# Routing attention with an FFN on one core: the checks of the row sums move behind the next turn's exponentials in the first batch

## The chip, the cores and the metric

The kernel runs on one core of a Trainium2 chip. The metric is the device time of one execution in microseconds (us), taken as the median of several runs; less is better. The profile shows one further execution, instruction by instruction. Engines are named as there: PE is TensorE (matrix products; PEld is its weight load), DVE is VectorE, ACT is ScalarE, POOL is GpSimd, SP is SyncE, whose queue issues nearly all DMA transfers. Each engine works through its own instructions in a fixed order and waits on semaphores for the others.

## The reference

Attention by clusters, for 4 batches of 8 heads, 768 positions and 64 dimensions, and then a two-layer network with a quick GELU on the 3072 rows of 512 values.

```python
q_assign = np.argmax(np.einsum('bhsd,hcd->bhsc', q_n, c_n), axis=-1)   # 16 centroids a head
k_assign = np.argmax(np.einsum('bhsd,hcd->bhsc', k_n, c_n), axis=-1)
mask = q_assign[:, :, :, None] == k_assign[:, :, None, :]
scores = np.where(mask, scale * np.matmul(q, k.transpose(0, 1, 3, 2)), -1e9)
attn = np.exp(scores - np.max(scores, axis=-1, keepdims=True))
attn = attn / (np.sum(attn, axis=-1, keepdims=True) + 1e-09)
x = np.matmul(attn, v)            # then (B,H,S,D) -> (B*S, H*D)
h = x @ w_in                      # 512 -> 2048
g = h * (1.0 / (1.0 + np.exp(-1.702 * h)))
out = g @ w_out                   # 2048 -> 512
```

The weights come as 64-bit floats, q, k, v and the centroids as 32-bit floats.

## The kernel before, in words

`fast` computes everything without subtracting the row maximum. To be safe it takes, for every group of rows, the reciprocals of the row sums and checks them: `check(g)` (L472) makes two ACT passes over the tile `rec` (128 x 384). The first copies it and adds it up (L476), the second applies a Relu with a bias and adds that up (L478). Both sums go to `sums`, which is read near the end; if a sum is out of bounds, `general` computes everything anew (L33 to L35).

**Groups and turns.** Two heads of one batch make a pair (16 pairs, four to a batch). Each pair has two halves of 384 query rows, so there are 32 groups g. A group takes six units u, one for each tile of 128 keys: `scores(u)` (L386, PE, 2 heads), `part(u)` (L398, the mask as a further product, in the first batch only), `exps(u)` (L412, ACT, L417), `mask(u)` (L420: in the first batch only POOL's running sum of the exponentials, L438; from the second batch on also DVE's masking, L428), `values(u)` (L442, PE, L449; after the sixth unit ACT copies the result at L454). Two units make a turn t, so a group has three turns (TG = 3) and a batch 24 (TB = 24). The loop over the turns (L597 to L638) writes the instructions out by hand, and that is the order in which each engine works.

**One turn t**, in the order of the code: the scores and `part` of its two units; their exponentials; in the second half of the first batch and later (`second_half`, t >= 12) one round of weight conversion (L609); `check` of whatever group has been normalised and not yet checked (L610, L611); `mask`; centroid products of a coming pair, if they are due (`prep_near`, whose ACT copy is L290); `values` of the turn before; every third turn (t = 4, 7, 10, 13, ...) `normalise(g)` for the group that has just been completed, before the preparation steps when t >= 12 (L625) and after them otherwise (L629); the preparation steps of coming pairs (`prep_turn`: three PE transposes at L270 and one ACT copy at L275 each; `prep_assign` on DVE, L295 to L324); the check again, when t < 24 (L630, L631); a round of weight conversion (L633); chunks of the network (`first`, L513, with tanh at L485 and a DVE product at L486; `second`, L491, with ACT's scaling at L496); and a further round (L638) in odd turns with t >= 12.

**Normalising** (L456): PE adds POOL's sums over the partitions with a product by ones (L461), DVE takes the reciprocal straight from PSUM (L464) and multiplies the group's result by it (L466). `rec` is one of three rotating tiles `short` that also hold the products of `prep_near` and a step of `prep_assign`.

**Weight conversion.** A round (L190) loads a chunk (L154, SP), splits another (DVE L167 and L169, then ACT L171 and L173) and joins the one before (DVE L179, L182, L185). There are 32 chunks, all in the first batch's stage.

**PSUM.** Three banks `m` rotate among the transposes, the centroid products, the row sums of L461, the network's chunks and its outputs (`bank()`, L106). Two double banks `s` hold the scores: the scores of a turn can't start before the exponentials of the turn before have read theirs.

**After the first batch** the same loop goes on for three batches, with chunks of the network as filling; then the rest of the network is computed with seven products instead of eight (L696 to L728).

Of the kernel before, what the change touches and what calls it, by code (L numbers as in the profile page):

```python
# [18 lines left out]
def kernel(  # L19
    tc: tile.TileContext,  # L20
    q: bass.AP,
    k: bass.AP,
    v: bass.AP,
    centroids: bass.AP,
    moe_w_in: bass.AP,
    moe_w_out: bass.AP,
    out: bass.AP,
):

    args = (q, k, v, centroids, moe_w_in, moe_w_out, out)
    bad = fast(tc, *args)  # L33
    with tc.If(bad > 0):
        general(tc, *args)  # L35
# [3 lines left out]
def fast(  # L39
# [150 lines left out]
    def round_next():  # L190
        i = w_done[0]
        if i < NW:
            load_w(i + 2)
            split_w(i)
        if 0 < i <= NW:
            join_w(i - 1)
        w_done[0] += 1
# [188 lines left out]
    def scores(u):  # L386
        g, kt = divmod(u, NJ)
        p, h = split(g)
        ps = ps_s.tile([P, 2, 512], FP32, name="s")
        for a in range(2):  # L390
            rows = slice(a * D, (a + 1) * D)
            nc.tensor.matmul(out=ps[:, a, 0:HALF],  # L392
                             lhsT=T[p, 1][rows, kt * P:(kt + 1) * P],
                             rhs=T[p, 0][rows, h * HALF:(h + 1) * HALF],
                             start=True, stop=(p >= HP))
        s_of[u] = ps[:, :, 0:HALF]

    def part(u):  # L398

        g, kt = divmod(u, NJ)  # L400
        p, h = split(g)
        if p >= HP:
            return
        for a in range(2):
            r = 32 * (2 * (p % 2) + a)
            nc.tensor.matmul(
                out=s_of[u][:, a, :],
                lhsT=hots[p // 2, 1][r:r + NC, kt * P:(kt + 1) * P],
                rhs=hots[p // 2, 0][r:r + NC, h * HALF:(h + 1) * HALF],
                start=False, stop=True)  # L410

    def exps(u):  # L412
        p, h = split(u // NJ)
        s = s_of[u]
        if p < HP:
            A_of[u] = ap.tile([P, 2, HALF], FP32, name="A")
        nc.scalar.activation(out=A_of[u] if p < HP else s, in_=s, func=AF.Exp,  # L417
                             scale=SCALE)

    def mask(u):  # L420

        g, kt = divmod(u, NJ)
        p, h = split(g)
        s = s_of.pop(u)
        if p >= HP:
            A_of[u] = ap.tile([P, 2, HALF], FP32, name="A")
            for a in range(2):
                nc.vector.scalar_tensor_tensor(  # L428
                    out=A_of[u][:, a, :],
                    in0=qcode[p][:, a, h * HALF:(h + 1) * HALF],  # L430
                    scalar=code[p][:, kt % NH, 1, kt // NH, a:a + 1],
                    in1=s[:, a, :], op0=ALU.is_equal, op1=ALU.mult)
        A = A_of[u]
        if kt == 0:
            return
        if kt == 1:
            sum_of[g] = ap.tile([P, 2, HALF], FP32, name="sum", bufs=2)
        nc.gpsimd.tensor_tensor(out=sum_of[g],  # L438
                                in0=A_of[u - 1] if kt == 1 else sum_of[g],
                                in1=A, op=ALU.add)  # L440

    def values(u):  # L442
        g, kt = divmod(u, NJ)
        p, h = split(g)
        if kt == 0:
            o_of[g] = ps_o.tile([P, 512], FP32, name="o")
        A = A_of.pop(u)
        for a in range(2):
            nc.tensor.matmul(out=o_of[g][a * D:(a + 1) * D, 0:HALF],  # L449
                             lhsT=v_in[p][:, a, kt, :], rhs=A[:, a, :],  # L450
                             start=(kt == 0), stop=(kt == NJ - 1))
        if kt == NJ - 1:
            O_of[g] = xp.tile([P, HALF], FP32, name="x")
            nc.scalar.copy(O_of[g], o_of.pop(g)[:, 0:HALF])  # L454

    def normalise(g):  # L456

        sm = sum_of.pop(g)
        ps = bank()
        for a in range(2):  # L460
            nc.tensor.matmul(out=ps[a * D:(a + 1) * D, 0:HALF], lhsT=ones,  # L461
                             rhs=sm[:, a, :], start=True, stop=True)
        rec = recs[g] = short()
        nc.vector.reciprocal(out=rec, in_=ps[:, 0:HALF])  # L464
        x = xT_of[g] = O_of.pop(g)
        nc.vector.tensor_tensor(out=x, in0=x, in1=rec, op=ALU.mult)  # L466
        if g % HP == HP - 1 and g < 2 * HP:
            (half_ffn, ffn)[g // HP].extend((ffn_half, ffn_tiles)[g // HP]())

    recs = {}  # L470

    def check(g):  # L472


        rec = recs.pop(g)
        nc.scalar.activation(out=rec, in_=rec, func=AF.Copy,  # L476
                             accum_out=sums[:, 0, g:g + 1])
        nc.scalar.activation(out=rec, in_=rec, func=AF.Relu, bias=top[:, 0:1],  # L478
                             scale=-2.0 * LIMIT * LIMIT,
                             accum_out=sums[:, 1, g:g + 1])  # L480
# [86 lines left out]
    TB = 2 * HP * TG  # L567

    prep_at = {}
    for p in range(1, NPAIR):  # L570
        b, hp = divmod(p, HP)
        for i in range(2 if p == 1 else 0, len(PREP)):
            if p == 1:
                t = (i - 2) // 2
            elif b == 0:
                t = (hp - 2) * TG + 1 + i // 2
            else:
                t = b * TB + TG * hp - (7, 7, 6, 6, 4, 3, 2)[i]
# [5 lines left out]
    def prep(p, i):  # L584
        if i == 0 and p:
            load_v(p)
        PREP[i](p)
        if i in (1, 3) and loads:
            load_qk(*loads.popleft())
# [7 lines left out]
    for t in range(NT + 2):  # L597
        us = range(2 * t, 2 * t + 2) if t < NT else ()
        for u in us:
            scores(u)  # L600
        if t == 0:
            prep(0, 6)
        for u in us:
            part(u)
        for u in us:
            exps(u)
        second_half = t >= TB // 2
        if second_half:
            round_next()  # L609
        if recs:  # L610
            check(*recs)  # L611
        for u in us:
            mask(u)
        work = sorted(prep_at.get(t, ()), key=lambda w: PREP[w[1]] != prep_near)
        while work and PREP[work[0][1]] == prep_near:
            prep(*work.pop(0))
        if 1 <= t <= NT:
            for u in range(2 * t - 2, 2 * t):
                values(u)

        todo = half_ffn or (ffn if len(ffn) > NF // 2 else ())
        owed += (rate if half_ffn else 0.62) if todo else -owed
        g = (t - 2) // TG if t >= 2 and (t - 2) % TG == TG - 1 else None
        if g is not None and second_half:
            normalise(g)  # L625
        for p, i in work:
            prep(p, i)
        if g is not None and not second_half:
            normalise(g)  # L629
        if recs and t < TB:  # L630
            check(*recs)  # L631
        if second_half or t and t % 4 != 3:
            round_next()  # L633
        while owed >= 1 and todo:
            todo.popleft()()
            owed -= 1
        if second_half and t % 2:
            round_next()  # L638
# [565 lines left out]
```

## Time and profile before

| what | value |
|---|---|
| median of 5 runs | 1081.89 us (1081.7 to 1084.53) |
| the profiled execution's own time | 1081.72 us |
| its span, first to last instruction | 1079.9 us |
| PE busy | 1028.3 us (95%) |
| DVE busy | 600.3 us (56%) |
| ACT busy | 359.5 us (33%) |
| POOL busy | 296.4 us (27%) |
| mean granted PE clock | 0.984 |
| check, first pass L476 (32 of them, whole span) | 0.52 us and 0.19 us to read its sum |
| check, second pass L478 | 0.62 us and 0.19 us |
| ACT's idle time before L476, waiting for L466, 40 to 216 us | 24.7 us in 7 waits |
| first seven checks, start of L476 | 44.23, 63.12, 77.47, 99.03, 133.25, 166.18, 207.88 us |

The span counts from the first to the last instruction; the execution's own time has 1.8 us around it. A share of busy time is an average over the whole span, and the first batch, which takes some 230 us, differs much from what follows. In a timeline, a row gives the start, the duration, the engine, the line, the operation, the tiles (out<-in) and in brackets how long the engine had been idle and what ended that. fp32 products appear as two records each. Where neighbouring rows overlap a little, instructions are pipelined.

### The profile page before, as it was taken

To read this page: it belongs to the slowest core of one execution; us is meant where nothing else is said; L and a number is where in the kernel's file an instruction comes from. 1 tells how busy PE (TensorE), PEld (TensorE's weight loads), DVE (VectorE), ACT (ScalarE), POOL (GpSimd) and SP (SyncE) were. 2 spreads that over 40 slices of the span, in tenths; PEclk is the share of its full clock that TensorE was granted. 3 is DMA by queue.
4 is the path that set the end of the run, shared out by engine and by line. 5 is a ranking of instruction groups with operands and counts; after the bars stand their busy time and mean duration, and the time that the engine had idled before them with its cause. 6 is when DMAs were issued, how large, how long until landed. Compare 5 with 4: busy or idle time off the path is not lost. (4 is left out here: it accounts for less than half of the span.)

```text
span 1079.9 us, 11138 instructions
## 1 busy us (share of the span) xinstructions
PE 1028.3 (95%) x4142; PEld 502.0 (46%) x4142; DVE 600.3 (56%) x912; ACT 359.5 (33%) x649; POOL 296.4 (27%) x168
## 2 busy tenths in 40 slices
PE   7878798999999999999998999999999999999997
PEld 3323354345544455444543455444555444555443
DVE  3899998326876787667877866400366200565000
ACT  3654464324545555555554122100122000122000
POOL 2555222224665657655667000000000000000000
PEclk9998899999999999999999999999999999999999
DMA  7523354112003310221000000000000000000000
GB/s 195 143 64 112 117 162 127 47 39 69 9 15 73 97 31 1 59 67 40 9 1 1 10 1 1 10 20 19 11 1 0 10 19 20 10 1 1 20 20 22
DMA packets 64817, 45.18 MB, mean 42 GB/s; under 512 B 51952, under 2 KB 57584, under 8 KB 64752
## 3 DMA queue, kind: packets, MB, share of 16 engines
q1 hardware_dynamic: 64608, 44.33, 14.3%
q8 instruction: 35, 0.57, 0.2%
q14 instruction: 30, 0.25, 0.1%
q10 hardware_dynamic: 144, 0.03, 0.0%
HBM read 38.04 MB, written 6.31 MB: 41 GB/s over the span
## 5 line engine op out<-in xcount | busy, mean ns | idle before, releaser
L438 POOL TENSOR_TENSOR sum<-sum,A 128x768 f32<-128x768 f32 x128 | 235.7, 1841 | 201.3 <-DVE A L428 104.5
L491 PE MATMUL m<-w_out,gb 128*128 128x512 f32 x576 | 247.7, 592 | 0.0
L708 DVE TENSOR_TENSOR gb<-b,gb 128x384 f32<-128x384 f32 x168 | 93.4, 556 | 214.9 <-PE b L703 208.3
L428 DVE SCALAR_TENSOR_TENSOR A<-qb,code,s 128x384 f32<-128x384 uint8 x288 | 157.6, 607 | 94.8 <-ACT s L417 79.7
L491 PEld LDWEIGHTS m<-w_out,gb 128*128 128x128 f32 x576 | 109.4, 190 | 137.1 <-issue 136.6
L392 PE MATMUL s<-T,T 64*128 64x384 f32 x768 | 158.8, 526 | 13.2 <-ACT A L417 9.0
L449 PE MATMUL o<-A,inv 128*64 128x384 f32 x768 | 146.9, 502 | 1.1 <-DVE A L428 1.1
L417 ACT ACTIVATE s<-s 128x768 f32<-128x768 f32 x144 | 109.4, 794 | 83.3 <-PE s L392 72.6
L392 PEld LDWEIGHTS s<-T,T 64*128 64x128 f32 x768 | 66.2, 189 | 86.4 <-issue 24.0
L496 ACT ACTIVATE y<-m 128x512 f32<-128x512 f32 x24 | 14.3, 596 | 261.6 <-PE m L491 238.6
L485 ACT ACTIVATE th<-gb 128x768 f32<-128x768 f32 x48 | 40.4, 842 | 170.0 <-DVE gb L708 140.0
L464 DVE RECIPROCAL short<-m 128x384 f32<-128x384 f32 x32 | 81.6, 2551 | 13.6 <-PE m L461 13.5
L449 PEld LDWEIGHTS o<-A,inv 128*64 128x64 f32 x768 | 47.1, 137 | 86.4 <-issue 81.2
L438 POOL TENSOR_TENSOR sum<-A 128x768 f32<-128x768 f32 x32 | 59.4, 1857 | 93.4 <-ACT A L417 43.9
L703 PE MATMUL b<-x,S 128*128 128x384 f32 x192 | 69.8, 486 | 0.0
L703 PE MATMUL b<-T,w_in 128*128 128x384 f32 x192 | 69.8, 486 | 0.0
L703 PE MATMUL b<-x,w_in 128*128 128x384 f32 x192 | 66.3, 486 | 0.0
L513 PE MATMUL m<-x,w_in 128*128 128x384 f32 x128 | 51.2, 558 | 15.7 <-ACT short L290 4.9
L491 PE MATMUL m<-w_out,g 128*128 128x512 f32 x120 | 58.6, 613 | 0.2 <-ACT T L275 0.2
L486 DVE SCALAR_TENSOR_TENSOR gb<-th,gb 128x768 f32<-128x768 f32 x48 | 45.7, 953 | 21.8 <-ACT th L485 21.8
L542 PEld LDWEIGHTS m<-x,w_in 128*128 128x128 f32 x384 | 44.7, 192 | 11.2 <-issue 10.2
L542 PE MATMUL m<-x,w_in 128*128 128x128 f32 x384 | 48.8, 280 | 0.5 <-ACT T L275 0.5
(95 smaller groups left out, 862.8 us busy)
## 6 DMA issues: line engine op xcount, KB each, us to landing
raw<-in_moe_w_in_dram SPq DMA_DIRECT2D x16, 512.0 KB, 3.7
raw<-in_moe_w_out_dram SPq DMA_DIRECT2D x16, 512.0 KB, 3.6
in<-in_q_dram SPq DMA_DIRECT2D x32, 192.0 KB, 2.9
in<-in_k_dram SPq DMA_DIRECT2D x32, 192.0 KB, 3.5
inv<-in_v_dram SPq DMA_DIRECT2D x16, 384.0 KB, 4.3
out_dram<-y SPq DMA_DIRECT2D x24, 256.0 KB, 2.0
qb<-line SPq DMA_DIRECT2D x12, 192.0 KB, 3.3
line<-row SPq DMA_DIRECT2D x12, 1.5 KB
```

The costliest lines, as they stand in the source:

```text
L392: nc.tensor.matmul(out=ps[:, a, 0:HALF], lhsT=T[p, 1][rows, kt * P:(kt + 1) * P], rhs=T[p, 0][rows, h * HALF:(h + 1) * HALF], start=True, ...
L417: nc.scalar.activation(out=A_of[u] if p < HP else s, in_=s, func=AF.Exp, scale=SCALE)
L428: nc.vector.scalar_tensor_tensor(out=A_of[u][:, a, :], in0=qcode[p][:, a, h * HALF:(h + 1) * HALF], scalar=code[p][:, kt % NH, 1, kt // NH ...
L438: nc.gpsimd.tensor_tensor(out=sum_of[g], in0=A_of[u - 1] if kt == 1 else sum_of[g], in1=A, op=ALU.add)
L449: nc.tensor.matmul(out=o_of[g][a * D:(a + 1) * D, 0:HALF], lhsT=v_in[p][:, a, kt, :], rhs=A[:, a, :], start=(kt == 0), stop=(kt == NJ - 1))
L464: nc.vector.reciprocal(out=rec, in_=ps[:, 0:HALF])
L486: nc.vector.scalar_tensor_tensor(out=g, in0=t, scalar=1.0, in1=h, op0=ALU.add, op1=ALU.mult)
L491: nc.tensor.matmul(out=ps[:, 0:DM], lhsT=g, rhs=w_out[:, f, :], start=(f == 0), stop=(f == NF - 1))
L513: nc.tensor.matmul(out=ps[:, 0:HALF], lhsT=w_in[:, c, f * P:(f + 1) * P], rhs=xT[c], start=(c == 0), stop=(c == NCH - 1))
L542: nc.tensor.matmul(out=ps[:, f % 2 * P:(f % 2 + 1) * P], lhsT=w_in[:, c, f * P:(f + 1) * P], rhs=xT[c][:, n * P:(n + 1) * P], start=(c == ...
L703: nc.tensor.matmul(out=ps[:, 0:HALF], lhsT=a(c), rhs=x(c), start=(c == 0), stop=(c == 1))
L708: nc.vector.tensor_tensor(out=o, in0=a, in1=b, op=ALU.add)
```

## The change

One condition and its call go. After it the check at L610 and L611 is the only one in the loop, so a group normalised in turn t is checked in turn t + 1, behind that turn's exponentials (and behind the round at L609, where there is one). Groups 7 to 31 were checked there already; groups 0 to 6, normalised in turns 4, 7, 10, 13, 16, 19 and 22, were checked in the turn of their normalisation.

```diff
@@ -627,8 +627,6 @@
             prep(p, i)
         if g is not None and not second_half:
             normalise(g)
-        if recs and t < TB:
-            check(*recs)
         if second_half or t and t % 4 != 3:
             round_next()
         while owed >= 1 and todo:
```

The lines behind it have numbers smaller by two in the changed kernel; line numbers in the text are those of the kernel before, unless a row of the changed kernel is shown.

## The prediction

> **What bounds the kernel now.** I read the page's slices first, then busy time by stretch, then the instructions of each engine in order of time from 40 to 220 us, where the moved checks stand. The slices: one digit is the busy share of 27 us in tenths.
>
> ```profile
> PE   7878798999999999999998999999999999999997
> DVE  3899998326876787667877866400366200565000
> PEclk9998899999999999999999999999999999999999
> ```
>
> PE is at 9 from the eighth slice (189 us) on. The seven slices before it are the only stage in which PE has slack, and in it DVE stands at 8 or 9 from the second slice on. All seven moved checks lie there (44.2 to 209.3 us). The stretches (columns: length, busy us and instructions of PE, PEld, DVE, ACT, POOL, granted clock, DMA share, GB/s):
>
> ```profile
> 137.20:172.60 35.40, 35.40 (x167) 17.78 (x166) 33.00 (x50) 21.46 (x41) 10.15 (x6) 1.00 0.48 146
> 172.60:177.60 5.00, 0.16 (x2) 0.00 (x0) 4.97 (x5) 2.21 (x5) 3.62 (x2) 0.98 0.36 105
> 177.60:184.50 6.90, 6.84 (x17) 3.94 (x18) 4.08 (x8) 2.50 (x6) 0.00 (x0) 0.77 0.84 239
> 217.00:1080.00 863.00, 845.05 (x3283) 418.35 (x3281) 434.69 (x677) 249.02 (x448) 218.71 (x121) 1.00 0.08 22
> ```
>
> PE's last long stop is 172.6 to 177.6, while DVE works without a pause; from 177.6 on PE is full and DVE is not. So the time is: how long DVE and ACT need until they let PE go at 177.6, and PE's own work after that. An earlier gain counts only if it shortens DVE's chain up to there; a delay of PE after that is paid in full.
>
> Four timelines (start, duration, engine, line, operation, and in brackets the idle time before with what ended it). ACT: the check of turn 7 with the exponentials of turn 8; the end of turn 20; turn 23.
>
> ```profile
> 59.53 0.81 ACT L364 ACTIVATE qb<-m 64x768 bf16<-64x768 bf16 x1
> 63.12 0.52 ACT L476 ACTIVATE short<-short 128x384 f32<-128x384 f32 x1 [2.77 <-DVE x L466]
> ...
> 64.29 0.19 ACT L478 ACTIVATION_READ_ACCUMULATOR short<-short,top 128x1 f32 x1
> 64.50 1.51 ACT L417 ACTIVATE A<-s 128x768 f32<-128x768 f32 x2
> ...
> 174.67 0.72 ACT L171 ACTIVATE e<-e,low 128x512 int32<-128x512 int32 x1 [1.57 <-DVE e L167]
> 176.61 0.63 ACT L173 ACTIVATE w_out<-w_out 128x512 f32<-128x512 int32 x1 [1.22 <-DVE w_out L169]
> 177.15 0.46 ACT L290 COPY short<-m 128x384 f32<-128x384 f32 x1
> ...
> 215.12 0.49 ACT L290 COPY short<-m 128x384 f32<-128x384 f32 x1
> ```
>
> ```profile
> 65.36 2.93 PE L392 MATMUL s<-T,T 64*128 64x384 f32 x8 [3.01 <-ACT A L417]
> ...
> 171.89 0.87 PE L270 MATMUL m<-ident,in 128*128 128x128 f32 x6
> 177.66 6.98 PE L513 MATMUL m<-x,w_in 128*128 128x384 f32 x16 [4.90 <-ACT short L290]
> ...
> 215.94 0.87 PE L270 MATMUL m<-ident,in 128*128 128x128 f32 x6
> ```
>
> ```profile
> 65.72 1.93 DVE L167 TENSOR_SCALAR e<-raw 128x512 int32<-128x512 int32 x1
> 67.57 2.04 DVE L169 TENSOR_SCALAR w_in<-raw 128x512 int32<-128x512 int32 x1
> ```
>
> ```profile
> 65.45 3.87 POOL L438 TENSOR_TENSOR sum<-sum,A 128x768 f32<-128x768 f32 x2 [2.78 <-ACT A L417]
> ```
>
> At 59.53 ACT has nothing more to do but the check, and the check waits for the reciprocal; the exponentials of turn 8, whose scores are ready at 60.9, stand behind it, and PE waits 3.01 us for them. That is the wait which the change takes away. The last two fences show a second coupling: L167 and L169 take 0.42 us elsewhere and 1.9 to 2.0 us beside a row sum of POOL. Between 44 and 177 us, 20 DVE instructions are lengthened so, by some 1.55 us each.
>
> **Moved.** Seven checks (turns 4, 7, 10, 13, 16, 19, 22), two ACT instructions each with their accumulator reads. Start to start a check takes ACT 1.26 us (44.23 to 45.49). Nothing is added or removed; the order of PE, DVE, POOL and the SP queue is unchanged. On ACT each check goes past the weight splits (L171, L173), tanh (L485) or output scaling (L496) at the end of its turn, and the next turn's exponentials; in turns 14, 17 and 20 also past one more split. It then stands before whatever follows.
>
> **The three early checks: gain taken as 0.** Turn 4: ACT can go on at once, but the next instruction, L171, waits for DVE's L167, which stands behind the same reciprocal (44.11 to 44.53). Exponentials of turn 5 start near 45.7, not 46.62. Then the check (1.26), two copies and the split come before those of turn 6. POOL's sums start 0.9 earlier too and now lengthen L167 and L169 (46.83) in place of L182 and L185, so L173 waits until 50.8, and the exponentials of turn 6 start near 51.35, not 50.72. Nothing is left of it. Turn 7: exponentials of turn 8 start near 60.95, not 64.50. POOL follows at 62.7, so the two DVE instructions from 63.05 on are the long ones; L173 is free at about 67.4, the exponentials of turn 9 start at 68.0, not 68.66, and PE, which has worked off everything by 65.8, waits its 3 us one turn later (scores of turn 10). The row-sum matmul L461 comes at 73.4 to 73.8 as against 73.35. Turn 10: exponentials of turn 11 about 1.0 earlier, but DVE has no pause between 74.2 and 104.3, so nothing comes of it. Bounds: DVE stands idle waiting for PE 1.14 us at 53.78 and 1.18 us at 74.22, so at best 2.3 is won; at worst POOL's sums that today meet an idle DVE or a reciprocal (those from 52.31, 58.95 and 72.97) meet weight instructions, 1.55 lost for each.
>
> **Turns 13, 16, 19: gain 0.33.** The one of turn 13 falls into 1.76 us in which ACT waits for L167 anyway (before 110.66). Turn 16: tanh comes 0.9 earlier and DVE saves 0.33 of idle time at 136.14, but its third gelu product (137.77) waits for a PE block that only the reciprocal releases, so that is given back; the check itself falls into the 1.96 us before 144.42. Turn 19: DVE saves 0.33 at 169.07 (idle for the tanh), and from there to L169 at 174.56 it has no pause: -0.33.
>
> **Turn 19's check in its new place: +1.26.** It now stands between L173 (176.61) and L290 (177.15). L290 empties the PSUM bank of the centroid products; there are three banks (m), the transposes at 171.89 hold the other two, and PE's next block, L513, waits for L290. Behind the check wait also the copies L275 and the split at 179.00, which have slack. PE pays 1.26.
>
> **Clock after the longer stop: +0.33.** The 16 records at 177.66 take 6.98 us; at the pace of 24 in 7.91 they would take 5.27 to 5.44 (other rows of 16: 5.33, 5.43), a loss of 1.55, at a granted clock of 0.77. Worked the same way, after stops of 2.4 to 4.2 us PE lost 1.6 (47.47), 1.4 (65.36), 1.7 (80.70), 1.75 (99.05), 3.0 (113.41) and 1.8 us (132.68): mean 1.88, which is 0.33 more than it loses here today; bounds -0.2 and +1.5. The Trainium skill ("TensorE: Matmul & The Clock Gate", What's actually happening) gives one busy window of about 3.4 us at half clock after an idle one; by it, as an estimate, 1.7 us are lost whatever the length of the stop, and the sum would be 0.2 lower. Its window of 3.4 us for the fall disagrees with this trace, where a stop of 2.36 us was enough.
>
> **Turn 22's check: +0.75.** It comes before L290 at 215.12, which then ends at 216.85, not 215.6. The trace names L290 as the last release of PE's weight load for L270 at 215.94. If the first transposes need that bank, PE waits 0.95; if only the second three do (they start at 216.4), 0.5. Between the two: 0.75. L513 at 177.66 shows that a bank behind L290 does hold PE.
>
> **Sum:** -0.33 + 1.26 + 0.33 + 0.75 = +2.0 us. The profiled execution took 1081.72 us (span 1079.9 and 1.8 around it): 1083.7. The median of the runs is 0.17 above that execution, so 1083.9 for the median.
>
> **Rivals.** 0.2% of the median, 2.16 us, is about what a measurement tells from no change: slower is above 1084.05, faster below 1079.7.
> Slower by more: POOL's sums, earlier by 0.9 to 3.5 us, lengthen DVE instructions in the early turns. For it: today five of ten sums from 47 to 77 us cost DVE nothing, which an earlier start can spoil. Against: DVE's idle 1.14 and 1.18 us take up part. It decides from one instruction (+1.55: 1085.4); two make 2.0 + 3.1, or 1087.0.
> Faster: DVE wins both idle stretches (2.3) and two long instructions slip under a reciprocal (2 x 1.55): 2.0 - 5.4 = -3.4, 1078.5. For it: reciprocals at 59.73 and 74.22 hide sums today. Against: those two are already used, and from 77 to 95 us every sum meets weight work, wherever it starts.
> No change: PE has slack after 177.66 that I don't see, and the two delays vanish, which leaves -0.33: 1081.6. For it: PE stands 1.01 us at 193.25. Against: that wait is for DVE's L304, which follows PE's own transposes and moves with them.
>
> **How the numbers follow.** Forecast 0.52, its own range 1083.2 (+1.3: clock -0.2, turn 22 at 0.55) to 1085.6 (+3.7: clock +1.5, turn 22 at 0.95, no 0.33): of it 0.29 above 1084.05, 0.23 below. Slower rival 0.22. No change 0.13. Faster 0.13, of which 0.02 ends within the bound. So slower 0.51, same 0.38, faster 0.11. The range 1080.9 to 1087.0 leaves out most of the faster case and the upper half of the slower one, 0.1 each.
>
> **What would show it.** Right: L476 between L173 and L290 near 177, L513 behind a stop of 5.5 to 6.2 us; L476 before L290 near 216 and a new PE stop of 0.5 to 1 there; PE's 3 us stop moved from turn 9 to turn 10; the reciprocals of turns 7 and 10 within 1 us of 59.7 and 74.2. Wrong: L169 of turn 20 ending more than 1.5 us away from 176.6 (then the early turns decide), or PE starting L513 before L290 ends.

## The result and the profile after

| | before | after |
|---|---|---|
| median | 1082.64 us (1079.37 to 1084.53, 56 runs) | 1084.39 us (1082.37 to 1086.72, 33 runs) |
| profiled execution: own time, span | 1081.72, 1079.9 us | 1082.8, 1080.9 us |

The ratio of after to before is 1.0017, 95% interval 1.0011 to 1.0022: by the ratio 1.84 us more (0.0017 of 1082.64, interval 1.2 to 2.4), by the two medians 1.75. The forecast was +2.0 us, 1083.9, and the range from 1080.9 to 1087.0 holds the result. In absolute terms the forecast is 0.5 us low, because its base, 1081.89, was the median of five executions, and 56 gave 1082.64. By the prediction's bound of 0.2% the change counts as "same", to which it had given 0.38, and not as "slower" (0.51); the interval shows all the same that it costs something.

The slices of the page after are those of before, but for a tenth here and there:

```profile
PE   7877697999999999999998999999999999999997
DVE  3899997326876788677877866400366200565000
PEclk9999898999999999999999999999999999999999
```

The same three kinds of stretch, taken at PE's last long stop (columns as before: length, busy us and instructions of PE, PEld, DVE, ACT, POOL, clock, DMA share, GB/s):

```profile
170.60:176.90 6.30, 0.10 (x1) 0.00 (x0) 6.20 (x7) 3.48 (x9) 3.67 (x2) 0.88 0.26 85
176.90:184.80 7.90, 7.79 (x16) 4.38 (x17) 2.96 (x6) 2.45 (x6) 0.00 (x0) 0.66 0.75 233
217.00:1080.90 863.90, 845.79 (x3286) 419.06 (x3286) 434.85 (x677) 249.76 (x450) 219.20 (x121) 1.00 0.08 22
```

PE's stop is 6.31 us where it was 4.90, the clock behind it was granted at 0.66, not 0.77, and from 217 us on PE has the same 98% as before. ACT's timeline after, at the three places that the prediction showed:

```profile
57.09 0.81 ACT L364 ACTIVATE qb<-m 64x768 bf16<-64x768 bf16 x1
58.41 1.51 ACT L417 ACTIVATE A<-s 128x768 f32<-128x768 f32 x2 [0.51 <-POOL sum L438]
60.68 0.52 ACT L476 ACTIVATE short<-short 128x384 f32<-128x384 f32 x1 [0.76 <-DVE x L466]
...
174.72 0.63 ACT L173 ACTIVATE w_out<-w_out 128x512 f32<-128x512 int32 x1 [1.22 <-DVE w_out L169]
175.26 0.51 ACT L476 ACTIVATE short<-short 128x384 f32<-128x384 f32 x1
...
176.50 0.46 ACT L290 COPY short<-m 128x384 f32<-128x384 f32 x1
...
216.73 0.46 ACT L290 COPY short<-m 128x384 f32<-128x384 f32 x1
```

and PE's:

```profile
59.84 1.56 PE L392 MATMUL s<-T,T 64*128 64x384 f32 x8
...
65.97 2.81 PE L392 MATMUL s<-T,T 64*128 64x384 f32 x8 [2.70 <-ACT A L417]
...
177.01 7.98 PE L513 MATMUL m<-x,w_in 128*128 128x384 f32 x16 [6.31 <-ACT short L290]
...
217.24 0.55 PE L270 MATMUL m<-ident,in 128*128 128x128 f32 x3 [0.41 <-ACT short L290]
```

The exponentials of turn 8 now start 1.3 us after L364 does, no longer behind the check; the scores of turn 9 (59.84) follow without a stop, and the stop is at those of turn 10 (65.97). In turn 20 the check stands between L173 and L290; in turn 23 the second three transposes wait for L290.

**How two single executions are laid side by side.** The first reciprocal of a row sum (L464) starts at 40.97 us before and at 38.53 after, with the same order of instructions up to there: the start alone differs by 2.44 us from execution to execution. So shifts are counted from that point, after less before:

| point | before | after | shift from the first reciprocal |
|---|---|---|---|
| second and third reciprocal | 59.73, 74.22 | 57.29, 71.70 | 0.00, -0.08 |
| third gelu product of turn 16 (L486) | 137.77 | 135.71 | +0.38 |
| end of L169, turn 20 | 176.58 | 174.68 | +0.54 |
| start of L290, turn 20 | 177.15 | 176.50 | +1.79 |
| start of L491, turn 20 | 184.48 | 184.83 | +2.79 |
| start of L491, turn 23 | 216.65 | 217.62 | +3.41 |

In this pair the parts are +0.54 up to the end of L169, +1.25 for the check, +1.00 for the 16 records of L513 behind the stop and +0.62 in turn 23. 3.41 less 2.44 is the 1.0 by which the spans differ. A pair shows where delays stand, not how large they are on average. From the first reciprocal to L491 of turn 20 the profile before took 143.51 us and the changed one 146.30, but the profiles with only three and only five early checks moved (below) took 146.07 and 145.90, without any check in front of L290. What a move is worth is therefore read from the ratios over many executions.

### The profile page after: what moved, and what is told of

It reads as the page before. It is cut to its first block, busy times and chain, and to the rows that moved or that the text cites. A ratio compares the mean times of both kernels' runs of the same rounds, so it can differ in the third digit from the quotient of the medians.

```text
span 1080.9 us, 11143 instructions
## 1 busy us (share of the span) xinstructions
PE 1024.0 (95%) x4142; PEld 501.0 (46%) x4142; DVE 601.0 (56%) x912; ACT 359.5 (33%) x649; POOL 294.6 (27%) x168
## 3 DMA queue, kind: packets, MB, share of 16 engines
HBM read 38.04 MB, written 6.31 MB: 41 GB/s over the span
## 5 line engine op out<-in xcount | busy, mean ns | idle before, releaser
L491 PE MATMUL m<-w_out,gb 128*128 128x512 f32 x576 | 247.7, 592 | 0.0
L491 PEld LDWEIGHTS m<-w_out,gb 128*128 128x128 f32 x576 | 109.4, 190 | 137.1 <-issue 136.6
L392 PE MATMUL s<-T,T 64*128 64x384 f32 x768 | 155.5, 516 | 13.7 <-ACT A L417 9.6
L392 PEld LDWEIGHTS s<-T,T 64*128 64x128 f32 x768 | 65.0, 186 | 85.5 <-issue 23.3
L464 DVE RECIPROCAL short<-m 128x384 f32<-128x384 f32 x32 | 81.6, 2551 | 12.6 <-PE m L461 12.5
L513 PE MATMUL m<-x,w_in 128*128 128x384 f32 x128 | 51.5, 560 | 18.5 <-ACT short L290 6.3
L491 PE MATMUL m<-w_out,g 128*128 128x512 f32 x120 | 59.0, 616 | 0.2 <-ACT T L275 0.2
L486 DVE SCALAR_TENSOR_TENSOR gb<-th,gb 128x768 f32<-128x768 f32 x48 | 45.7, 953 | 21.8 <-ACT th L485 21.8
```

What stands on the lines that cost most here:

```text
L392: nc.tensor.matmul(out=ps[:, a, 0:HALF], lhsT=T[p, 1][rows, kt * P:(kt + 1) * P], rhs=T[p, 0][rows, h * HALF:(h + 1) * HALF], start=True, ...
L486: nc.vector.scalar_tensor_tensor(out=g, in0=t, scalar=1.0, in1=h, op0=ALU.add, op1=ALU.mult)
L491: nc.tensor.matmul(out=ps[:, 0:DM], lhsT=g, rhs=w_out[:, f, :], start=(f == 0), stop=(f == NF - 1))
L513: nc.tensor.matmul(out=ps[:, 0:HALF], lhsT=w_in[:, c, f * P:(f + 1) * P], rhs=xT[c], start=(c == 0), stop=(c == NCH - 1))
```

## Experiments

Each ratio is against the kernel before on the same chip, with its 95% interval. Line 630 is the condition of the removed check.

**The three early checks alone.**

```diff
-        if recs and t < TB:
+        if recs and 10 < t < TB:
```

> Only the checks of turns 4, 7 and 10 are moved. My theory: the earlier exponentials gain nothing, because the next waits (weight splits behind lengthened DVE work, PE's stop one turn later) take their place: ratio to before 1.0000, between 0.9994 and 1.0006, and the reciprocal of turn 10 (L464) keeps its distance to that of turn 4 within 0.2 us of the 33.25 us in the kernel before. Rival 'collisions': these moves lengthen DVE work and are the cause of the loss: ratio 1.0015 or more, that distance 1.5 us longer. Rival 'gain': PE's removed stops count: ratio below 0.9985.

Measured: 0.9994 (0.9983 to 1.0005). The distance from the first to the third reciprocal is 33.16 us, against 33.25 before. These three moves don't cause the loss, and a gain, if there is one, can't be told from none.

**The check of turn 19 alone.**

```diff
-        if recs and t < TB:
+        if recs and t < TB and t != 19:
```

> Only the check of turn 19 is moved, to turn 20, where it stands between L173 and the copy L290. My theory: PE's stop before L513 in turn 20 becomes 1.0 to 1.3 us longer and the slow clock after it costs up to 1.5 more: ratio 1.0015, between 1.0008 and 1.0025. Rival: the bank behind L290 has slack and the loss comes from other moves: ratio 1.0000, at most 1.0005.

Measured: 1.0013 (1.0002 to 1.0024). Here L513 stood behind a stop of 5.74 us, against 4.90 before, and its 16 records took 8.38 us. The stop is 0.84 us longer and not the 1.0 to 1.3 expected, and with only early checks moved it was 5.49 and 5.50, so the stop of one profile doesn't size the cost. What doesn't scatter: L290 starts 0.54 us after L173 in all five profiles with no check between them (before, three early, turn 22, behind the copy, five early) and 1.78 us after it in the three with the check (after, turn 19, both late), and PE's L513 starts 0.51 us after L290 in each of them. So there is a loss with this one move; its interval alone would still let the rival's 1.0005 pass, and the run of both late checks below decides that.

**The check of turn 22 alone.**

```diff
-        if recs and t < TB:
+        if recs and t < TB and t != 22:
```

> Only the check of turn 22 is moved, to turn 23, before the copy L290. My theory: the second three transposes L270 of that turn wait 0.4 to 0.6 us for L290, paid in full: ratio 1.0005, between 1.0002 and 1.0009; L270 in turn 23 split by a stop. Rival: nothing there: 1.0000 and no stop.

Measured: 1.0002 (0.9986 to 1.0017), too wide for 0.5 us. The profile decides only whether the wait is there. PE's timeline of this kernel:

```profile
219.45 0.55 PE L270 MATMUL m<-ident,in 128*128 128x128 f32 x3 [0.41 <-ACT short L290]
```

The split and the wait of 0.41 us are there, as in the changed kernel, and not in the kernel before, where the six transposes run in one piece of 0.87 us. What this move alone costs over many executions isn't shown.

**Both late checks, and the five others.** Two kernels that divide the change between them.

```diff
-        if recs and t < TB:
+        if recs and t < 18:
```

> Only the checks of turns 19 and 22 are moved. My theory: they carry the whole loss: ratio to before 1.0019, between 1.0010 and 1.0030. Rival 'collisions' (the five early moves carry it): at most 1.0005.

```diff
-        if recs and t < TB:
+        if recs and 18 < t < TB:
```

> Only the checks of turns 4, 7, 10, 13 and 16 are moved. My theory: nothing or a small gain, as with the first three alone and with all seven behind the copy: ratio 0.9994, between 0.9984 and 1.0004. Rival 'collisions': 1.0010 or more.

Measured: 1.0022 (1.0009 to 1.0035) for the two, 0.9996 (0.9983 to 1.0010) for the five: 2.4 us and -0.4 us, together about what the whole change costs. The checks of turns 19 and 22 carry the loss.

**All seven moved, but behind the copy L290.**

```diff
-        if recs:
+        if recs and t > TB:
             check(*recs)
...
             prep(*work.pop(0))
+        if recs and t < TB:
+            check(*recs)
```

> All seven checks are moved as in the change, but in their new turn they stand behind the copy L290 instead of before it. My theory: the loss goes, since L290 is no longer delayed in turns 20 and 23: ratio to before 1.0000, between 0.9993 and 1.0006. Rival 'collisions' (the earlier exponentials lengthen DVE work): the loss stays, ratio 1.0012 or more.

Measured: 0.9984 (0.9974 to 0.9995), a miss on the good side: the loss goes, and 0.05 to 0.26% less than before remains. On ACT this kernel differs from the changed one only in turns 20 and 23, by the order of check and L290 (L290 stands in no other of the turns to which a check moved). Its slowest execution (1082.22) is faster than the fastest of the changed kernel (1082.37), and the medians are 3.4 us apart. So the place of these two checks is shown to make the loss. Where the gain against the kernel before comes from isn't shown: the runs with three and with five early moves lie at 0.9994 and 0.9996, and their intervals overlap with this one.

**More ACT time at the same place.** The changed kernel with four copies of the tile `rec` onto itself before the check of turn 20.

```diff
         rec = recs.pop(g)
+        for _ in range(4 if g == 5 else 0):
+            nc.scalar.activation(out=rec, in_=rec, func=AF.Copy)
```

> The changed kernel, with four copies of one reciprocal tile onto itself on ACT just before the moved check of turn 20 (some 0.37 us each, 1.5 us in all, work that changes no value). My theory: ACT time before L290 in turn 20 is paid in full by PE: the stop before L513 is 1.5 us longer than in the changed kernel and the ratio to before is 1.0031, between 1.0022 and 1.0042. Rival: L290 has slack and PE is bound elsewhere: the ratio stays at that of the changed kernel, 1.0017, at most 1.0021.

ACT's and PE's timelines of this kernel (its lines behind L475 have numbers larger by two, so L477 is the added copy and L515 is L513):

```profile
175.79 0.63 ACT L173 ACTIVATE w_out<-w_out 128x512 f32<-128x512 int32 x1 [1.22 <-DVE w_out L169]
176.33 2.17 ACT L477 ACTIVATE short<-short 128x384 f32<-128x384 f32 x4
...
179.79 0.46 ACT L290 COPY short<-m 128x384 f32<-128x384 f32 x1
```

```profile
180.30 8.37 PE L515 MATMUL m<-x,w_in 128*128 128x384 f32 x16 [8.54 <-ACT short L290]
```

Measured: 1.0036 (1.0023 to 1.0048). The copies took 2.2 us, not the 1.5 that I had reckoned from other copies; PE's stop is 2.23 us longer than in the changed kernel (8.54 less 6.31), and the ratio is 0.0019, or 2.1 us, above that kernel's. ACT time before L290 is paid one to one by PE's stop, and by the whole time as nearly as the intervals can tell.

**The weight round and the check behind the preparation.** The changed kernel; in turns 20 and 23 the centroid copy and the transposes' copies come right behind the exponentials.

```diff
+        work = sorted(prep_at.get(t, ()), key=lambda w: PREP[w[1]] != prep_near)
+        late = second_half and t < TB and work and PREP[work[0][1]] == prep_near
-        if second_half:
+        if second_half and not late:
             round_next()
-        if recs:
+        if recs and not late:
             check(*recs)
...
-        work = sorted(prep_at.get(t, ()), key=lambda w: PREP[w[1]] != prep_near)
...
         for p, i in work:
             prep(p, i)
+        if late:
+            round_next()
+            check(*recs)
```

> The changed kernel, but in turns 20 and 23 the weight round and the check come behind the preparation steps, so that on ACT the copies L290 and L275 come right behind the exponentials. My theory: PE's stop before L513 in turn 20 is set by ACT's wait for L169 in front of L290, so it falls from 5 us or more to 1 or 2 us, the slow clock behind it goes too, and the ratio to before is 0.9955, between 0.9935 and 0.9975. Rival: DVE's chain sets PE's progress in another way (the next tanh or weights): 0.9985 or more.

Measured: 0.9943 (0.9923 to 0.9963), 6.2 us less than before and faster than both kernels (six executions). ACT and PE of this kernel in turn 20:

```profile
171.49 1.49 ACT L417 ACTIVATE A<-s 128x768 f32<-128x768 f32 x2
172.87 0.48 ACT L290 COPY short<-m 128x384 f32<-128x384 f32 x1
173.23 0.88 ACT L275 COPY T<-m 128x384 f32<-128x384 f32 x2
174.56 0.72 ACT L171 ACTIVATE e<-e,low 128x512 int32<-128x512 int32 x1 [0.45 <-DVE e L167]
176.52 0.63 ACT L173 ACTIVATE w_out<-w_out 128x512 f32<-128x512 int32 x1 [1.23 <-DVE w_out L169]
177.05 0.51 ACT L476 ACTIVATE short<-short 128x384 f32<-128x384 f32 x1
```

```profile
173.40 5.43 PE L513 MATMUL m<-x,w_in 128*128 128x384 f32 x16 [0.93 <-ACT short L290]
```

L171 and L173 wait for DVE as ever, but the copies that PE needs no longer stand behind them. PE's stop is 0.93 us, and its 16 records run at the full pace of 5.43 us.

**The same with the checks left in their old place.** The kernel before with the first and the last part of that edit, without the lines on the check.

> The kernel before, its checks where they were, with the weight round of turns 20 and 23 behind the preparation steps as in the run e10. My theory: what counts is only what stands before L290 and L275 on ACT, so with these in front it is all the same whether the checks are moved: ratio to before 0.9945, between 0.9925 and 0.9965, PE's stop before L513 in turn 20 at most 2 us. Rival: the moved checks bring part of the gain of that run: 0.9970 or more.

Measured: 0.9956 (0.9942 to 0.9970), 4.8 us less than before; PE's stop before L513 is 0.76 us, and the 16 records take 5.43 us. With L290 and L275 in front, no difference between moved and unmoved checks can be told (0.9943 and 0.9956, the intervals overlap by more than half of their length).

**Only L290 in front.** The changed kernel with the centroid products and their copy before the round; the copies L275 stay behind round and check.

```diff
+        work = sorted(prep_at.get(t, ()), key=lambda w: PREP[w[1]] != prep_near)
+        while t < TB and work and PREP[work[0][1]] == prep_near:
+            prep(*work.pop(0))
         second_half = t >= TB // 2
         if second_half:
             round_next()
...
-        work = sorted(prep_at.get(t, ()), key=lambda w: PREP[w[1]] != prep_near)
```

> The changed kernel with only the centroid products and their copy L290 moved in front of the weight round in turns 13 to 23; the copies L275 stay behind round and check. My theory: PE gets the bank for its first block L513 early, but the second block needs a bank that L275 empties behind L169, L173 and the check, so part of the stop comes back in the middle of the two blocks: ratio to before 0.9980, between 0.9960 and 1.0000. Rival: L290 alone is what PE waits for: 0.9955 or less.

PE of this kernel in turn 20:

```profile
171.67 2.85 PE L513 MATMUL m<-x,w_in 128*128 128x384 f32 x8 [0.93 <-ACT short L290]
177.07 2.85 PE L513 MATMUL m<-x,w_in 128*128 128x384 f32 x8 [2.55 <-ACT T L275]
```

Measured: 0.9977 (0.9965 to 0.9988). The first block gets its bank after 0.93 us; the second waits 2.55 us for the bank that L275 empties. So both copies matter: L290 gives back the bank of the first block and L275 that of the second, in ACT's order.

## Why the prediction was right, step by step

**PE's last long stop divides the time: right.** In the pair the stop grew by 1.41 us (4.90 to 6.31); the two kernels in which it fell to 0.93 and 0.76 us are 6.2 and 4.8 us faster than before. One reading beside it was wrong: not all seven moved checks lie in the seven slices with slack. That of turn 22 (207.88) lies in the eighth (189 to 216), where PE is at 9, which fits the price that it got.

**Turns 4, 7 and 10, gain 0: right in sum, and partly by luck.** Counted from the first reciprocal, the second and third came within 0.08 us of where they were. Turn 4: the exponentials of turn 6 start at 48.84, that is 51.28 on the scale of before, where 51.35 was reckoned. L167 and L169 are the long ones now, as DVE's timeline after shows:

```profile
44.38 1.92 DVE L167 TENSOR_SCALAR e<-raw 128x512 int32<-128x512 int32 x1
46.23 2.04 DVE L169 TENSOR_SCALAR w_in<-raw 128x512 int32<-128x512 int32 x1
...
159.41 2.19 DVE L185 TENSOR_TENSOR w_out<-w_out,e 128x512 f32<-128x512 f32 x1
```

Turn 7: the exponentials of turn 8 start at 60.85 on that scale (60.95 reckoned), and PE's stop went from turn 9 to turn 10 (2.70 us after 3.01). One wait took the other's place. But the profiles of all runs show two effects that the sum didn't have. In the seven with these three checks moved, the third reciprocal comes 32.2 to 33.2 us after the first, in the five others 33.3 to 34.8. And in the same seven one instruction of turn 19, the last row of the fence above, takes 2.19 or 2.20 us; in the five others it takes 0.69, as before:

```profile
161.47 0.69 DVE L185 TENSOR_TENSOR w_out<-w_out,e 128x512 f32<-128x512 f32 x1
```

So the collision that the rival 'slower by more' named, set to 0 in the sum, did come once, with the early moves; how these reach turn 19 wasn't followed. It wasn't paid in full: the 0.34 us that DVE had waited before the reciprocal behind it are gone, and L466 takes 0.56 us instead of 1.05. At the end of L169 in turn 20 the seven stand 135.7 to 137.0 us after the first reciprocal and the five 135.3 to 138.2, which tells no difference, and neither do the ratios of the early moves.

**Turns 13, 16 and 19, gain 0.33: not seen as a net gain.** The saving at the tanh of turn 19 is there: the shift from the first reciprocal is +0.96 at the last L185 before it (166.57 after, 168.05 before) and +0.56 at the gelu product behind it (167.19 and 169.07), 0.4 less. But the 0.96 had been lost before: 0.38 in turn 16, where PE's block ran slower behind its stop (4.88 us, not 4.54), and the rest by the long L185 of turn 19. The first isn't shown to belong to the change: in the kernel with only the two late checks moved, where the order was still that of before, the same block took 4.86 us.

**Turn 19's check, +1.26: right.** From the start of L173 to that of L290 are 1.78 us after and 0.54 before: 1.24. The run with this check alone gave 1.4 us (0.2 to 2.6), and the one with four copies more shows that each further us there is a us of PE's stop.

**The clock, +0.33: within its bounds, not settled.** In the pair it was +1.00 (7.98 less 6.98). Over the profiles, the 16 records took 6.98, 8.46, 7.38, 7.45 and 8.38 us behind stops of 4.9 to 5.5 us (before, three early, turn 22, behind the copy, five early: mean 7.73), and 7.98, 8.38, 8.25 and 8.37 behind 5.7 to 8.5 (after, turn 19, both late, four copies: mean 8.25): 0.5 more. With a scatter of 1.5 among the first five this doesn't show that a longer stop costs more.

**Turn 22's check, +0.75: a little too much.** In the pair it was 0.62. The trace's release at the weight load of the first transposes, from which the middle between 0.5 and 0.95 came, was no wait: only the second three needed the bank.

**The signs.** L476 stands where it was said in turns 20 and 23. The stops are just outside what was said: 6.31 us, not 5.5 to 6.2, and 0.41, not 0.5 to 1. Taken literally, the sign of being wrong was there: L169 of turn 20 ended at 174.68, 1.9 us from 176.6, and the reciprocals came 2.4 and 2.5 us early, where 1 us was allowed. That is the earlier start of this execution (2.44 us, before any check had moved); the prediction hadn't allowed for it, and counting from the first reciprocal was chosen afterwards.

In the runs the two late checks cost 2.4 us (1.0 to 3.8), for which the sum had 2.0 (1.26, 0.33 and 0.75, less the 0.33 of turn 19), and the other five -0.4 (-1.8 to +1.1), for which it had 0. So the mechanism of the loss was right; that the sum came within 0.2 us is luck, since its single terms scatter by up to 1.6 us from execution to execution. The rival 'slower by more' fell with the runs of the early checks, 'no change' with the run of four copies, 'faster' with the result. The gain that could be had was in the stop that the prediction had named as the one that sets the time, not in the waits that the change took away.

## What to carry to other kernels

Before moving work behind something on an in-order engine, look at what will stand behind it in its new place, and who waits for that: here 1.26 us of checking moved in front of a copy that empties the PSUM bank which PE needs next. A wait taken away in a stage that another engine bounds is replaced by the next wait; look for the last stop of the engine that bounds the rest and for what stands before the instruction that ends it. Here clearing that place gave 4.8 to 6.2 us, where the change cost 1.8. And a single pair of profiles can mislead by more than the effect: price a move by the ratios of many executions.

## What the runs showed of the hardware

After stops between 2.3 and 3.4 us PE ran on sometimes slowly and sometimes not: 2.81 us for eight records of L392 after 2.70 us (changed kernel), 2.73 after 2.36 (before), but 1.62 after 3.36 (four copies), and 2.85 for eight of L513 after 2.55 (the copy L290 in front), which is the full pace. After stops of 4.9 us and more the 16 records of L513 were slow in all nine profiles that have such a stop, by 1.5 to 3.0 us, and the length of the stop didn't order them.

One and the same stop can cost differently. Behind the 3.01 us before the scores of turn 9, the kernel before (first row) and the one with only turn 22's check moved (second row), whose order is still the same there, ran these products:

```profile
68.65 1.51 PE L449 MATMUL o<-A,inv 128*64 128x384 f32 x8
```

```profile
68.56 2.77 PE L449 MATMUL o<-A,inv 128*64 128x384 f32 x8
```

The clock granted from 65 to 70 us was 0.68 in the first and 0.50 in the second, and this is the 1.6 us by which the third reciprocal comes later there (34.83 us after the first, not 33.25); DVE's instructions between them take the same time in both. The time to the first reciprocal differs by up to 2.6 us (38.41 to 40.97 among the profiles).
